# Two of four weight sums moved from VectorE to GpSimd, and two groups of loads moved along the sync queue, in an attention and MLP kernel

## Chip, cores and metric

The kernel runs on one core of one Trainium2 chip. The time is device microseconds of one execution. Executions are marked fast or slow: slow means over 1.5% above the fastest of the same kernel. A profiled execution also has a span, from its first to its last instruction, some 1.7 us below its time.

## The reference, cut to what matters

Eight batches ("groups") of 8 heads, 576 queries of 64, keys and values averaged over 8 rows; softmax; then an MLP with a tanh GELU over all 4608 tokens.

```python
k_p = k.reshape(B, H, Sp, 8, D).mean(axis=3)         # Sp = 72
v_p = v.reshape(B, H, Sp, 8, D).mean(axis=3)
attn = softmax(scale * q @ k_p.T)                    # 576 x 72 a head
x = (attn @ v_p) ... reshape(4608, 512)
h = x @ w_in                                         # 512 x 2048
g = 0.5 * h * (1 + tanh(c * (h + 0.044715 * h**3)))
out = g @ w_out                                      # 2048 x 512
```

## The kernel before

TensorE runs one MLP of 512 tokens after another: groups 0 to 6, then the "remainder" (64 tokens of each group), then group 7. I call these steps 0 to 8. While step n runs, ScalarE, VectorE and GpSimd prepare the attention of the group of step n+1, and the sync queue loads the group after that. Work is placed by hooks: `at(hooks, s, f)` calls f just before the s-th matmul of a step, and each engine runs its instructions in the order of these calls.

From step 1 on, the second half of the MLP is a fast 2x2 block product with 7 products in place of 8. It needs four sums of blocks of w_out, made once, the first at the end of step 0 and the others at the start of step 1, and sums of the activations in each step:

```python
def w_sums(which, m0, m1, eng):
    b11, b12, b21, b22 = [wq[:, m0:m1, i, HN * h:HN * h + HN] for i in range(2) for h in range(2)]
    t = [tw[:, i, m0:m1] for i in range(4)]
    in0, in1 = [(b12, b11), (b22, t[0]), (b22, b12), (b21, t[1])][which]
    eng.tensor_tensor(out=t[which], in0=in0, in1=in1, op=ALU.subtract)    # L405, 128x2048 bf16
```

What stands beside it on VectorE, and the loads:

```python
def pool(b, c0, c1):                        # averages K or V: three additions a call, L147 to L149
    ...
def finish(g, r, o, eng):                   # step 0's result out of PSUM, which frees a bank
    ...
    copy(eng, osb, o); store(g, r, osb)
# sync queue, within a step:
#   keys' transpose (L199), queries' transpose (L220), loads, four weight transposes eT (L294)
at(hooks, nj, norm, n, j, nc.gpsimd if j == 1 else nc.vector)
at(hooks, nj, e_transpose_dma, n, j)
...
at(hooks, 64 + 105, values, n, [nc.scalar, nc.vector])      # TensorE needs all four eT here, L326
```

PSUM holds TensorE's results, in banks that are copied out before TensorE uses them again. The sums of the activations are L411 to L414, the softmax is L252 (row sums), L261, L267. L360 and L472 are the two matrix products, L236 the scores, L421 the first matmuls of a step.

The softmax here doesn't subtract the row's maximum and nothing guards it: scores larger than these inputs give would overflow.

## Time and profile before

The median of the three runs was 286.09 us (285.46 to 286.67). The profile that came with them: 289.0 us, span 287.3. The table gives the length of the steps, as the distance between the first weight loads of L421 in TensorE's timeline, and TensorE's waits within them.

| profile of before (slow) | from start | step 1 | step 2 | step 3 | steps 4 and 5 |
|---|---|---|---|---|---|
| length, us | 52.06 | 30.32 | 30.66 | 29.53 | 28.43 each |
| TensorE's waits, us | | 0.82 scores, 1.02 values | 1.77 values | half clock | none |

A step without waits takes 28.43 us. The lines that carry this are in the prediction.

### The profile page before, as it was taken

Reading aid. Unit: us, or ns where it says so; the run is one execution under the profiler, and the core shown is the slowest. Engines: PE = TensorE matmul, PEld = TensorE weight load, DVE = VectorE, ACT = ScalarE, POOL = GpSimd, SP = SyncE. Lnnn points to the kernel's source line nnn. Section 1 sums busy time; section 2 is a strip of 40 time slices with the busy share of each in tenths; the row PEclk is TensorE's granted clock in tenths of the full one; section 3 lists DMA queues with packets and bytes.
Section 4 is the critical chain, followed back from the end, with each engine's and each line's share of the span. In section 5 each row is a group of like instructions: output and inputs, shape, how many; then the busy total and the mean of one; then the engine's idle time right before and its main releaser. Section 6 shows DMA issues by size and latency. Waiting matters only on the chain.

```text
span 287.3 us, 6029 instructions
## 1 busy us (share of the span) xinstructions
PE 276.0 (96%) x2430; PEld 176.4 (61%) x2430; DVE 200.2 (70%) x361; ACT 168.2 (59%) x264; POOL 58.1 (20%) x91
## 2 busy tenths in 40 slices
PE   8889999998989997999999999999999999999994
PEld 3678844446844683448745864586458845864583
DVE  4882868987867984499679966996699435844521
ACT  1586574787446852676467646763776377637620
POOL 4740272002400340031203120312031200100000
PEclk9999999999999998999999999999999999999999
DMA  7999999999989998696689868946813730253013
GB/s 227 303 186 281 373 385 179 325 328 258 197 236 255 308 175 192 216 347 73 157 221 349 131 158 222 283 55 154 235 48 43 168 104 0 48 119 75 1 40 111
DMA packets 71759, 54.34 MB, mean 189 GB/s; under 512 B 45618, under 2 KB 57906, under 8 KB 71730
## 3 DMA queue, kind: packets, MB, share of 16 engines
q1 hardware_dynamic: 69474, 51.72, 70.2%
q0 software_dynamic: 2112, 2.10, 4.6%
q8 instruction: 19, 0.31, 0.5%
q10 hardware_dynamic: 144, 0.13, 0.1%
q14 instruction: 10, 0.08, 0.1%
HBM read 36.70 MB, written 9.44 MB: 161 GB/s over the span
## 4 chain that ended last, share of the span: by engine, by line
PE 78%; DMA 4%; DVE 3%; issue 1%
PE mm L360 32%; PE mm L472 31%; PE mm L421 5%; PE xo L326 3%; PE x L472 2%; DMA eT<-eb 2%; PE sc L236 2%; DMA qT<-q_b 2%; DVE eb L267 1%; DVE den L252 1%; PE xo L335 1%; PE mm L376 0%; DVE r L261 0%; DVE kv L147 0%; DVE kv L148 0%
## 5 line engine op out<-in xcount | busy, mean ns | idle before, releaser
L360 PE MATMUL mm<-xT,w_in_b 128*128 128x512 bf16 x448 | 98.0, 379 | 0.0
L362 ACT ACTIVATE gT<-mm 128x512 bf16<-128x512 f32 x112 | 66.9, 598 | 27.8 <-PE mm L360 27.7
L360 PEld LDWEIGHTS <-w_in_b 128*128 128x128 bf16 x448 | 43.7, 98 | 52.9
L472 PEld LDWEIGHTS <-gT 128*128 128x128 bf16 x512 | 48.5, 98 | 10.4 <-issue 2.5
L169 POOL TENSOR_TENSOR vbd<-kvb,vmask 128x256 bf16<-128x256 bf16 (+2 forms) x40 | 23.0, 597 | 96.6 <-DVE kvb L149 55.7
L472 PEld LDWEIGHTS <-stage 128*128 128x128 bf16 x384 | 37.5, 98 | 4.4
L411 DVE TENSOR_TENSOR stage<-gT 128x512 bf16<-128x512 bf16 (+1 forms) x31 | 15.6, 503 | 21.4 <-ACT gT L362 21.2
L472 PE MATMUL mm<-tw,gT 128*128 128x256 bf16 x240 | 30.4, 276 | 0.0
L472 PE MATMUL mm<-w_out_b,gT 128*128 128x256 bf16 x240 | 29.9, 273 | 0.0
L88 ACT CAST xT<-xo 128x1024 bf16<-128x1024 f32 (+1 forms) x11 | 10.2, 935 | 32.7 <-PE xo L326 28.0
L252 DVE TENSOR_REDUCE den<-e 128x8 f32<-128x576 f32 x36 | 26.5, 736 | 3.2 <-ACT e L245 2.9
L88 ACT COPY osb<-mm 128x512 f32<-128x512 f32 x30 | 17.6, 588 | 17.3 <-PE mm L472 17.0
L472 PE MATMUL mm<-tw,stage 128*128 128x256 bf16 x224 | 26.7, 273 | 0.0
L147 DVE TENSOR_TENSOR kv<-kv 128x1024 f32<-128x1024 f32 (+3 forms) x19 | 21.3, 1119 | 7.6 <-DMA kv<-in_k_dram 5.1
L245 ACT ACTIVATE e<-sc 128x576 f32<-128x576 f32 x36 | 21.8, 649 | 6.0 <-PE sc L236 4.4
L267 DVE TENSOR_TENSOR eb<-e,r 128x576 bf16<-128x576 f32 x25 | 20.8, 831 | 0.9
L412 DVE TENSOR_TENSOR gT<-gT 128x512 bf16<-128x512 bf16 (+1 forms) x31 | 14.6, 470 | 8.9 <-ACT gT L362 7.6
L90 DVE CAST xT<-xo 128x1024 bf16<-128x1024 f32 (+1 forms) x9 | 10.0, 1106 | 15.0 <-PE xo L326 11.4
L267 POOL TENSOR_TENSOR eb<-e,r 128x576 bf16<-128x576 f32 x7 | 8.1, 1150 | 56.5 <-ACT e L245 56.5
L90 POOL CAST q_b<-q_sb 128x1024 bf16<-128x1024 f32 (+1 forms) x13 | 13.6, 1067 | 20.1 <-DMA q_sb<-in_q_dram 20.0
L421 PE MATMUL mm<-xT,w_in_b 128*128 128x512 bf16 x64 | 16.3, 400 | 0.1
L371 PE MATMUL mm<-xT,w_in_b 128*128 128x256 bf16 x128 | 15.6, 273 | 0.1
(84 smaller groups left out, 288.9 us busy)
## 6 DMA issues: line engine op xcount, KB each, us to landing
kv<-in_k_dram SPq DMA_DIRECT2D x7, 1024.0 KB, 6.7
q_sb<-in_q_dram SPq DMA_DIRECT2D x7, 1024.0 KB, 11.3
kv<-in_v_dram SPq DMA_DIRECT2D x6, 1024.0 KB, 9.4
out_dram<-osb SPq DMA_DIRECT2D x12, 512.0 KB, 3.0
kv<-in_v_dram SPq DMA_DIRECT2D x4, 512.0 KB, 10.8
w_in_b<-in_moe_w_in_dram POOLq DMA_DIRECT2D x4, 512.0 KB, 6.7
w_out_s<-in_moe_w_out_dram SPq DMA_DIRECT2D x2, 1024.0 KB, 13.7
stage<-in_moe_w_out_dram SPq DMA_DIRECT2D x2, 1024.0 KB, 14.9
```

The costliest lines, as they stand in the source:

```text
L88: eng.copy(out=out, in_=in_)
L90: eng.tensor_copy(out=out, in_=in_)
L147: add(out=t[:, :, 0:4, :], in0=t[:, :, 0:4, :], in1=t[:, :, 4:8, :], op=ALU.add)
L169: eng.tensor_tensor(out=vbd[p0:128, b, n0:n1, :].rearrange("p (c r) (hh d) -> p c (r hh) d", c=max(m, 1), d=D), in0=kvb[p0:128, 4 + c0:4 + ...
L245: nc.scalar.activation(out=e.rearrange("p (x h) s -> p x (h s)", x=2), in_=sc[:, :, 0:4 * Sp], func=ACT.Exp, scale=1.0 / 64.0)
L252: nc.vector.reduce_sum(out=den, in_=e, axis=AX.X)
L267: eng.tensor_tensor(out=o.rearrange("p (pr hh s) -> p hh pr s", hh=2, s=Sp), in0=e.rearrange("p (hh pr) s -> p hh pr s", hh=2), in1=r.rear ...
L360: nc.tensor.matmul(out=hp, lhsT=w_in_b[:, ko, fo * 128:(fo + 1) * 128], rhs=st[g]["xT"][:, ko, :], start=(i == 0), stop=(i == KO - 1))
L362: nc.scalar.activation(out=gT[:, fo, :], in_=hp, func=ACT.Gelu_apprx_tanh)
L371: nc.tensor.matmul(out=hp[:, f, :], lhsT=w_in_b[:, ko, (fo + f) * 128:(fo + f + 1) * 128], rhs=st[g]["xT"][:, ko, c0:c0 + 256], start=(ko ...
L421: nc.tensor.matmul(out=hp[f], lhsT=w_in_b[:, ko, f * 128:(f + 1) * 128], rhs=st[g]["xT"][:, ko, :], start=(ko == 0), stop=(ko == 3))
L472: nc.tensor.matmul(out=xs[p] if acc is xs else acc[:, p, :], lhsT=lt, rhs=rt, start=bool(fresh and m == 0 and (p == 0 or (last and acc is ...
```

## The change

Its intent: VectorE is busy without a break where the four sums stand, and its work leads to the scores and values of step 1; two sums go to GpSimd, which is idle there. The queries' transpose of group 3 stood behind a load of V in the sync queue; V goes behind it. Two of the remainder's small query loads leave step 2.

```diff
     at(hooks, 185, w_sums, 0, 0, NP, nc.vector)
+    at(hooks, 187, w_sums, 2, 0, NP, nc.gpsimd)
 ...
         if n_ == 1:
-            for i in range(1, 4):
-                at(hooks, i, w_sums, i, 0, NP, nc.vector)
+            at(hooks, 1, w_sums, 1, 0, NP, nc.vector)
+            at(hooks, 2, w_sums, 3, 0, NP, nc.gpsimd)
 ...
                 at(hooks, 45, load_kv, n2, (0,))
-                at(hooks, 64 + 52, load_kv, n2, (1,))
+                at(hooks, 64 + 100, load_kv, n2, (1,))
 ...
-        if 2 <= n_ <= 5:
-            at(hooks, 58, load_q, R, n_ - 2, n_ - 1, nc.sync)
+        for j in {3: (0,), 4: (1, 2), 5: (3,)}.get(n_, ()):
+            at(hooks, 58, load_q, R, j, j + 1, nc.sync)
```

## The prediction

> **What bounds the kernel now.** I read the page first: TensorE is busy 96% of the span, and no other engine is near it.
>
> ```profile
> PE 276.0 (96%) x2430; PEld 176.4 (61%) x2430; DVE 200.2 (70%) x361; ACT 168.2 (59%) x264; POOL 58.1 (20%) x91
> PEclk9999999999999998999999999999999999999999
> ```
>
> So a change off TensorE can win only TensorE's gaps. The kernel runs one MLP per group, and the next group's attention is prepared beside it; I call these steps. In the chain that ended last, in order of time, the quiet steps 4 and 5 (142.84 to 171.27, 171.27 to 199.70) take 28.43 us each. Steps 1 and 2 are longer (52.28 to 82.68 is 30.40, 82.68 to 113.25 is 30.57). The chain names the gaps in them (start, length, what):
>
> ```profile
> 62.66 4.80 DMA qT<-q_b
> 67.46 0.04 issue
> 67.51 0.46 PE sc L236 x32
> ...
> 71.29 8.29 PE mm L472 x75
> 79.58 1.02 issue
> 80.60 1.18 PE xo L326 x16
> ...
> 106.78 2.59 DMA eT<-eb
> 109.37 1.50 issue
> 110.87 1.18 PE xo L326 x16
> ```
>
> The reader is to see three waits: 0.82 us before the scores at 67.51 (for the transposed queries), 1.02 us before the values at 80.60, and 1.77 us before the values at 110.87 (TensorE's timeline gives 0.82, 1.02 and 1.77). Both values waits end just after the last transposed weights land: issued at 77.80 and 108.10, each 2.6 us to landing in the view of that line. The windows view shows a second price of the longest gap:
>
> ```profile
> 108.82:112.24 3.42, 1.65 (x22) 0.55 (x20) 0.16 (x2) 0.35 (x1) 0.00 (x0) 1.00 0.76 207
> 112.24:115.65 3.41, 3.41 (x13) 1.57 (x11) 3.34 (x4) 1.25 (x2) 0.00 (x0) 0.50 1.01 233
> ```
>
> After 3.42 us in which TensorE was busy only 1.65, the clock (third figure from the end) was 0.50 for 3.41 us. That costs half of 3.41, 1.7 us. All that this change can win is therefore 1.02 + 1.77 + 1.7 and perhaps 0.82, together 5.3 us of 286, below 2%.
>
> The weight sums stand on VectorE's timeline (start, length), and the evidence on what GpSimd does to VectorE is in the last two lines and GpSimd's before them:
>
> ```profile
> 49.06 0.97 POOL L169 TENSOR_TENSOR vbd<-kvb,vmask 128x256 bf16<-128x256 bf16 x2 [1.41 <-DVE kvb L149]
> ...
> 50.10 1.21 DVE L405 TENSOR_TENSOR tw<-w_out_b 128x2048 bf16<-128x2048 bf16 x1
> 51.61 0.69 DVE L90 COPY osb<-mm 128x512 f32<-128x512 f32 x1 [0.30 <-PE mm L376]
> 52.22 1.22 DVE L405 TENSOR_TENSOR tw<-w_out_b,tw 128x2048 bf16<-128x2048 bf16 x1
> ...
> 73.11 1.15 POOL L267 TENSOR_TENSOR eb<-e,r 128x576 bf16<-128x576 f32 x1 [6.24 <-ACT e L245]
> ...
> 73.87 1.01 DVE L267 TENSOR_TENSOR eb<-e,r 128x576 bf16<-128x576 f32 x1
> 75.88 0.76 DVE L267 TENSOR_TENSOR eb<-e,r 128x576 bf16<-128x576 f32 x1
> ```
>
> **What the Trainium skill says.** (1) "SBUF — State Buffer", Who interferes with whom: a VectorE instruction with two SBUF inputs contends with a GpSimd instruction that reads SBUF, and the one that issues first holds the shared ports for its whole length. The trace agrees: VectorE's product at 73.87 took 1.01 against 0.76, as if it began 0.25 later, at 74.11, about 0.15 before GpSimd's (73.11 + 1.15 = 74.26) ended. (2) "GPSIMD Engine Reference", 3.1 Elementwise: two-input work on GpSimd takes about twice VectorE's time (4497 against 2293 ns at 2048 fp32). This trace gives less: in the groups by form the 128x576 product takes 1150 ns and the undisturbed 128x256 spread 612, so 1.68 ns an element and 0.18 fixed. (3) "DMA: Bandwidth & Descriptors", Two DMAs through the same engine are not ordered: within a queue descriptors start in order. Here the landings follow the issues of the sync queue, so a small transpose waits for loads ahead of it. (4) "TensorE: Matmul & The Clock Gate", Part 1: the clock halves after an idle window of 3.4 us; the 0.50 for 3.41 us above agrees, though here 48% busy was already too little.
>
> **Part 1: two weight sums to GpSimd.** VectorE loses 2 x 1.22 = 2.44 us (the instructions at 53.35 and 54.49). GpSimd gains two of 0.18 + 2048 x 1.68 ns = 3.6 us each; it is idle from 50.03 to 58.65, so its own time is free. The question is the lock.
> - The third sum needs only the converted weights, done at 45.5, so it starts when GpSimd is free, at about 50.0, some 0.1 before VectorE's first sum at 50.10. It holds the ports to 50.0 + 3.6 - 0.15 = 53.45. VectorE's first sum then ends at 53.45 + 1.21 = 54.66 and not 51.31. Behind it stands the copy at 51.61, which frees the PSUM bank that TensorE wants at 54.00: it now ends near 55.3, and TensorE stalls 1.3 us.
> - The second sum follows, to 56.4. The fourth needs it and is ready at about 56.45, when VectorE's first pooling addition (1.49 us, at 55.62 before) has just begun, to 57.8. The fourth takes the ports at 57.67, to 61.13. The second addition ends at 61.96, the pooled keys are done at 62.8, against 58.86 before.
> - From there: four product sums to 65.4 (2.6 us), V's pooling to 67.8 (2.4), the spread keys to 68.7, eight product sums (3.4) to 72.1. The softmax begins at 72.1 against 70.31, since some 1.9 us of VectorE's idle time is used up. The last transpose lands 1.75 later, at 82.15. TensorE reaches the values at 79.58 + 1.3 + 0.3 and waits about 1.1 again. **Step 1 ends 1.75 later.**
> - If VectorE wins the first race instead, its first sum is undisturbed, the second is blocked to 54.63, and the rest goes alike with no bank stall: 1.2 later. I take **+1.4**.
>
> **Part 2: V of group 3 behind the query transpose.** Before, the sync queue went like this (start, length of issuing):
>
> ```profile
> 79.08 0.59 SPq L108 DMA_DIRECT2D kv<-in_v_dram  x1
> 79.77 0.45 SPq L392 DMA_DIRECT2D out_dram<-osb  x1
> 80.32 7.01 SPq L220 DMA_TRANSPOSE qT<-q_b  x1
> ...
> 92.04 0.51 SPq L120 DMA_DIRECT2D q_sb<-in_q_dram  x1
> 92.59 5.05 SPq L124 DMA_DIRECT2D q_r<-in_q_dram  x2
> 101.15 8.18 SPq L294 DMA_TRANSPOSE eT<-eb  x4
> ```
>
> The transpose blocked the queue 7.01 us behind V, against 2.93 to 3.40 in other steps, and the loads of group 4 went out from 89.57. Now the transpose takes some 3 us, V follows at once (7.1 us to landing before), and the loads of group 4 are issued about 1.9 earlier against TensorE's work. V lands near 92.3, and VectorE pools it at 91.68 + 1.4 = 93.1: narrow, no wait.
>
> **Part 3: the remainder's queries from step 3 on.** The two that leave step 2 stood just ahead of its transposes: issued at 92.6 and 96.5, landed 13.6 and 10.2 later, at 106.2 and 106.7, and the first transpose at 107.3 though issued at 101.15. The queue issued the last one at 108.10 although its data was there at 105.63 (74.80 to 75.88 is the same run of instructions in step 1). Without them (1.0 us of the queue) and with part 2 (0.9), the last transpose can be issued when its data is ready and lands before TensorE asks. **Step 2 loses its gap: -1.77.** The half clock after it goes too. The gate looks at fixed windows of 3.41 us, so a gap of 1.77 fills enough of one in perhaps half of the executions, an estimate: 0.5 x 1.7 = **-0.8** in the median. Step 4 gets four of these small loads where it had two. Its first transpose landed at 165.5, the last at 168.9, and TensorE came at 169.28: 0.4 of slack against 1 us more in the queue, partly hidden: **+0.3**. Steps 3 and 5 keep what they have.
>
> Sum: 286.09 + 1.4 - 1.77 - 0.8 + 0.3 = 285.2.
>
> **Rivals.** (a) The ports are not held against VectorE so long, or GpSimd starts late enough. Then VectorE gains up to 2.4 us in step 1, the 1.02 us wait shrinks to 0.3 (the transposes also stand behind K of group 3, landing at 77), and the total is 286.1 - 0.7 - 1.8 - 0.8 + 0.3 = 283.1. That the change was thought worth making speaks for it; the 1.01 against 0.76 above speaks against. (b) The blocked VectorE stalls TensorE long enough to halve its clock in step 1 as well, 1.7 us more, and V lands late for its pooling: about 287. A stall of 1.3 is below the 1.77 that did it. (c) The transfers are only rearranged and the step 2 gap stays in part: 286 to 287; against it, 1 us of loads really leaves the queue ahead of the transposes.
>
> **Range and chances.** The rivals span 283.1 to 287, the spread of the runs is 1.2 us: 282.7 to 287.0. Faster by 2% would need 5.7 us, more than all gaps that the parts touch; slower by 2% needs two clock losses on top of my worst sum. Hence 0.03, 0.95, 0.02.
>
> **What would show it.** GpSimd's two sums of about 3.6 us from 50.0; VectorE's first or second sum, and a pooling addition, stretched by 2 to 3.4 us; TensorE idle near 54; the values of step 1 later than 80.60. In step 2: a query transpose issued in about 3 us, the last transpose landing before TensorE's values, no gap there and no 0.50 after it. I am wrong if VectorE's sums and additions keep their 1.2 and 0.8 us, or if step 2 keeps a gap over 0.5 us.

## The result, and the profile after

The changed kernel takes 289.26 us (288.34 to 290.11, 4 runs); the kernel before, in the same rounds, 286.38. Ratios are the mean time of one kernel's fast runs over that of the other's of the same rounds, so not quite the ratio of the medians: 1.0104, with a 95% interval of 1.0061 to 1.0147. The change costs 3 us, and the time lies outside my range of 282.7 to 287.0. The profile is of a fast execution (288.34 us, span 286.6).

First TensorE's timeline (start, length, what, and in brackets the idle time before it and what ended it): steps 1 and 2.

```profile
55.47 12.25 PE L360 MATMUL mm<-xT,w_in_b 128*128 128x512 bf16 x55 [1.62 <-DVE osb L90]
69.82 0.45 PE L236 MATMUL sc<-kbd,qT 64*64 64x72 bf16 x32 [1.67 <-DMA qT<-q_b]
81.47 1.16 PE L472 MATMUL mm<-tw,gT 128*128 128x256 bf16 x9 [0.56 <-DVE osb L457]
83.28 1.18 PE L326 MATMUL xo<-eT,vbd 32*64 32x512 bf16 x16 [0.66 <-issue]
...
111.71 1.18 PE L326 MATMUL xo<-eT,vbd 32*64 32x512 bf16 x16
```

Step 1 has four waits, 4.51 us together, where in the slow profile of before it had two of 1.84. Step 2 has none. The steps are now 33.32, 28.42, 28.42 and 28.43 us. Next GpSimd's and VectorE's timelines of step 1's beginning:

```profile
49.67 4.07 POOL L405 TENSOR_TENSOR tw<-w_out_b 128x2048 bf16<-128x2048 bf16 x1
56.63 5.25 POOL L405 TENSOR_TENSOR tw<-w_out_b,tw 128x2048 bf16<-128x2048 bf16 x1 [2.89 <-DVE tw L405]
```

```profile
49.78 5.04 DVE L405 TENSOR_TENSOR tw<-w_out_b 128x2048 bf16<-128x2048 bf16 x1
54.74 0.68 DVE L90 COPY osb<-mm 128x512 f32<-128x512 f32 x1
...
57.99 4.57 DVE L148 TENSOR_TENSOR kv<-kv 128x640 f32<-128x640 f32 x1
...
73.88 0.75 DVE L252 TENSOR_REDUCE den<-e 128x8 f32<-128x576 f32 x1
```

The reader is to see the two long VectorE instructions, which took 1.21 and 0.82 before. The first began 0.11 after GpSimd's sum and ended 1.08 after it, so it began its own 1.2 us of work only when GpSimd was nearly done. The copy at 54.74, which frees the PSUM bank, came next, and TensorE waited for it from 53.85 to 55.47. The second is the addition that GpSimd's other sum overtook: that sum shows 5.25 us, of which about 1.2 was its own waiting for the addition before.

Last the sync queue of step 2, which did as the prediction said: the queries' transpose is issued in 3.29 us and not 7.01, V behind it.

```profile
82.52 3.29 SPq L220 DMA_TRANSPOSE qT<-q_b  x1
85.86 0.57 SPq L108 DMA_DIRECT2D kv<-in_v_dram  x1
...
90.21 0.57 SPq L108 DMA_DIRECT2D kv<-in_k_dram  x1
```

From one profile of each kernel the account would read: step 1 +3.00, steps 2 and 3 -3.35, and 0.3 less before step 1, so the changed kernel's span is 0.7 us shorter. Its time is 3 us longer. One of the two profiles cannot be typical, and the first question for the chip was which.

### The profile page after: what moved, and what is told of

Same layout as the page of the kernel before. It is cut to its first block, busy times and chain, and to the rows that moved or that the text cites. A ratio compares the mean times of both kernels' runs of the same rounds, so it can differ in the third digit from the quotient of the medians.

```text
span 286.6 us, 6011 instructions
## 1 busy us (share of the span) xinstructions
PE 273.7 (95%) x2412; PEld 176.0 (61%) x2430; DVE 206.8 (72%) x359; ACT 168.2 (59%) x264; POOL 67.5 (24%) x93
## 4 chain that ended last, share of the span: by engine, by line
PE 79%; DVE 17%; issue 2%; ACT 0%; DVEq 0%; POOL 0%; POOLq 0%
PE mm L360 29%; PE mm L472 29%; PE mm L371 5%; PE mm L421 4%; PE x L472 2%; DVE kv L148 2%; DVE den L252 2%; PE xo L326 2%; DVE tw L405 2%; DVE eb L267 2%; PE warm L571 2%; PE sc L236 2%; DVE kv L147 2%; DVE eb L279 1%; DVE stage L411 1%
## 5 line engine op out<-in xcount | busy, mean ns | idle before, releaser
L360 PE MATMUL mm<-xT,w_in_b 128*128 128x512 bf16 x440 | 97.6, 379 | 2.0 <-DVE osb L90 1.6
L169 POOL TENSOR_TENSOR vbd<-kvb,vmask 128x256 bf16<-128x256 bf16 (+2 forms) x40 | 23.6, 612 | 84.9 <-DVE kbd L90 44.4
L88 ACT COPY osb<-mm 128x512 f32<-128x512 f32 x30 | 17.6, 588 | 15.9 <-PE mm L472 15.5
L267 DVE TENSOR_TENSOR eb<-e,r 128x576 bf16<-128x576 f32 x25 | 21.7, 867 | 0.9
L148 DVE TENSOR_TENSOR kv<-kv 128x512 f32<-128x512 f32 (+3 forms) x19 | 16.1, 849 | 0.7
```

The lines of the kernel that those rows point to most:

```text
L88: eng.copy(out=out, in_=in_)
L148: add(out=t[:, :, 0:2, :], in0=t[:, :, 0:2, :], in1=t[:, :, 2:4, :], op=ALU.add)
L169: eng.tensor_tensor(out=vbd[p0:128, b, n0:n1, :].rearrange("p (c r) (hh d) -> p c (r hh) d", c=max(m, 1), d=D), in0=kvb[p0:128, 4 + c0:4 + ...
L267: eng.tensor_tensor(out=o.rearrange("p (pr hh s) -> p hh pr s", hh=2, s=Sp), in0=e.rearrange("p (hh pr) s -> p hh pr s", hh=2), in1=r.rear ...
L360: nc.tensor.matmul(out=hp, lhsT=w_in_b[:, ko, fo * 128:(fo + 1) * 128], rhs=st[g]["xT"][:, ko, :], start=(i == 0), stop=(i == KO - 1))
```

## The experiments

**The theory.** GpSimd's sums hold VectorE off (a VectorE instruction that starts beside one does its own work only when that one ends) for their whole length; step 1 lengthens by 3 us; the gain of the moved loads in step 2 is not in ordinary executions. **The rival.** The moved loads do the harm: V of group 3 comes late, or four small loads in step 4 delay its transposes.

**1. The kernel before, once more.** No edit.

> The kernel before, once more, for a second profile of it. Ratio 1.000 within 0.004. What is asked is step 2 (from the start of one MLP to the start of the next): if the 1.77 us wait before the values of step 2 is in ordinary executions too, this profile shows step 2 at about 30.2 us (28.43 + 1.77) and step 3 at 28.4 when the clock is not halved. If that wait belonged to the one slow profile, step 2 is 28.4 to 29.4, and the gain that I promised to parts 2 and 3 was never there.

Measured: ratio 0.9987 (0.9965 to 1.0009), the profile fast, 284.35 us. Step 1 is 29.67 us, step 2 is 28.43. TensorE's timeline:

```profile
66.93 0.46 PE L236 MATMUL sc<-kbd,qT 64*64 64x72 bf16 x32 [0.90 <-DMA qT<-q_b]
...
79.30 1.18 PE L326 MATMUL xo<-eT,vbd 32*64 32x512 bf16 x16 [0.29 <-issue]
...
107.72 1.18 PE L326 MATMUL xo<-eT,vbd 32*64 32x512 bf16 x16
```

The wait of 1.77 us in step 2 is not there, nor the half clock after it. They belonged to the one slow profile. The queries' transpose stood behind V here too and was issued in 6.49 us (7.01 in the slow profile), so this long issue does not by itself make TensorE wait. What I meant to win in step 2 was, in this execution, nothing.

**2. Part 1 alone, and 3. parts 2 and 3 alone.** The edits are the first two and the last two places of the diff above.

> Only the two weight sums go to GpSimd; the loads stay as in the kernel before. Theory (GpSimd's long two-input instructions hold VectorE off): step 1 takes 33.0 to 33.6 us against 30.3, VectorE's first sum about 5.0 us and its second pooling addition about 4.6 us, ratio 1.009 to 1.018. Rival (the moved loads did the harm): ratio below 1.004 and step 1 under 31.5.

> Only the loads are moved; all four weight sums stay on VectorE. Theory: step 1 stays at 30.3 us and step 2 is 28.4 without a gap; ratio 0.994 if step 2's 1.77 us wait is there in ordinary executions of the kernel before, 1.000 if it is not. Rival (the moved loads did the harm): ratio above 1.004.

Measured: part 1 alone 1.0121 (1.0097 to 1.0145), step 1 33.31 us. Parts 2 and 3 alone 0.9982 (0.9963 to 1.0001), step 1 29.81. The product of the two, 1.0103, is the whole change's 1.0104. The rival falls: the harm is part 1. Parts 2 and 3 are within noise of nothing; by the interval they win 1.1 us at most. They did not even keep step 2 free of waits, though no remainder's query was in its way:

```profile
108.71 1.18 PE L326 MATMUL xo<-eT,vbd 32*64 32x512 bf16 x16 [0.69 <-DMA eT<-eb]
```

This wait scatters with either order of loads. With the old one it was 1.77, 0, 0.47 (part 1 alone), 0.75 (experiment 8) and 0 (experiment 11); with the new one 0, 0.69, 0.90, 0, 0.29, 0.65 and 0 (the changed kernel and experiments 3 to 7 and 10). The means are 0.60 and 0.36, from single profiles, the slow one among them; without it the old order has 0.31.

**4. The copy that frees the bank, on ScalarE.**

```diff
-            finish(g, r, o[r], nc.scalar if r == 3 else nc.vector)
+            finish(g, r, o[r], nc.scalar if r >= 2 else nc.vector)
```

> The changed kernel, with the third copy of step 0's result (the one that stood behind VectorE's held first sum and freed TensorE's PSUM bank) on ScalarE. If the lateness of step 1 is VectorE's chain, the 1.6 us stall at the start of step 1 goes but the waits for queries, sums and values grow by nearly as much: step 1 at 32.3 to 33.0 us, 0.3 to 1.0 less than the changed kernel's 33.3. If the stall itself is what costs, the whole 1.6 is won: step 1 at 31.7 us.

Measured: ratio 1.011 (1.0088 to 1.0133), step 1 32.83 us. The stall of 1.62 is gone, and the wait before the scores grew from 1.67 to 2.69:

```profile
68.89 0.63 PE L236 MATMUL sc<-kbd,qT 64*64 64x72 bf16 x32 [2.69 <-DMA qT<-q_b]
```

By these two profiles 0.5 us of step 1 hung on the stall itself; the times do not show it (1.011 against 1.0104). The rest is VectorE's lateness, which TensorE meets at the next place that needs it. The wait is put down to a DMA, but VectorE stands behind it: its copy L162 ended at 62.81, the keys' transpose was issued at 62.84, and the queries' transpose only behind that in the queue, at 64.50, though ScalarE's last conversion of the queries had ended at 62.16.

**5. GpSimd writes only.** Each of its sums is replaced by two fills with zeros of the same tile. The result is wrong.

```diff
-    at(hooks, 187, w_sums, 2, 0, NP, nc.gpsimd)
+    for _ in range(2):
+        at(hooks, 187, nc.gpsimd.memset, tw[:, 2], 0.0)
```

(The fourth sum likewise, with `tw[:, 3]`.)

> The changed kernel, but GpSimd, in place of each of the two sums, writes zeros twice into the same tile: it writes and reads nothing of SBUF. The result is wrong on purpose. If VectorE is held because both instructions READ through the shared interface, VectorE's first sum is back at 1.2 us and its second pooling addition at 0.8, step 1 takes 29.2 to 29.8 us and the ratio is 0.994 to 1.000. If any long GpSimd instruction beside VectorE does it (or the mere order of the instructions), step 1 stays above 31 us.

Measured: ratio 0.9992 (0.9965 to 1.0019), step 1 30.19 us. GpSimd's four fills ran from 49.54 to 56.82 without a break. GpSimd's line, VectorE's and then TensorE's timelines:

```profile
49.54 7.28 POOL L658 MEMSET tw<- 128x2048 bf16 x4
```

```profile
49.67 1.21 DVE L405 TENSOR_TENSOR tw<-w_out_b 128x2048 bf16<-128x2048 bf16 x1
...
54.87 1.49 DVE L147 TENSOR_TENSOR kv<-kv 128x1280 f32<-128x1280 f32 x1 [1.83 <-DMA kv<-in_v_dram]
56.39 0.82 DVE L148 TENSOR_TENSOR kv<-kv 128x640 f32<-128x640 f32 x1
```

```profile
67.12 0.45 PE L236 MATMUL sc<-kbd,qT 64*64 64x72 bf16 x32 [0.83 <-DMA qT<-q_b]
...
80.07 1.18 PE L326 MATMUL xo<-eT,vbd 32*64 32x512 bf16 x16 [0.87 <-DMA eT<-eb]
```

Two things follow. VectorE is not held by 7.3 us of GpSimd instructions that only write, so the hold comes with GpSimd's reading. And this kernel is part 1 at its best: VectorE is rid of two sums and of every hold in this stretch, and nothing is won that can be told from noise (by the interval 1.0 us at most). It stands 1.83 us before its first pooling addition, which waits for a load, and 1.04 before it copies the transposed keys; TensorE's two waits (0.83 and 0.87) are no shorter than in experiment 1 (0.90 and 0.29). Both name a transfer. Step 1 missed my 29.2 to 29.8, I take it for that reason.

**6. The same two sums in eight pieces each.**

```diff
-    at(hooks, 187, w_sums, 2, 0, NP, nc.gpsimd)
+    for m in range(NP):
+        at(hooks, 187, w_sums, 2, m, m + 1, nc.gpsimd)
```

(The fourth sum likewise.)

> The changed kernel, but each of GpSimd's two sums cut into eight of 128x256 (about 0.65 us each, so more GpSimd time in all). If the ports are held for one whole instruction at a time and then go to the other engine that waits, no VectorE instruction is held longer than about 0.6 us: no stall at the start of step 1, step 1 at 30.6 to 31.8 us, ratio 1.002 to 1.006. If it is GpSimd's total time that VectorE loses, step 1 stays at 33.

Measured: ratio 1.0063 (1.0042 to 1.0084), step 1 31.84 us, at the upper edge of the expectation. VectorE's timeline:

```profile
49.99 1.64 DVE L405 TENSOR_TENSOR tw<-w_out_b 128x2048 bf16<-128x2048 bf16 x1
...
56.40 1.17 DVE L148 TENSOR_TENSOR kv<-kv 128x640 f32<-128x640 f32 x1
...
58.48 0.61 DVE L162 COPY kvb<-kvb 128x320 bf16<-128x320 bf16 x1
```

Each VectorE instruction is held by part of a piece (0.43 and 0.35 us in the first two lines in place of 3.83 and 3.75), the stall at the bank is gone. The two engines take turns, instruction by instruction: the ports are held for one instruction and then go to the one that waits. But the pieces took GpSimd 17.6 us in all, with its waiting, and VectorE's two-input instructions pay again and again; the last line shows that a copy with one input pays too (0.61 us in place of 0.26). So it is still slower than doing the sums on VectorE.

**7. Only the third sum on GpSimd, and 10. only the fourth.** In the first, `nc.gpsimd` of `w_sums, 3` becomes `nc.vector`; in the second, the third sum goes back to VectorE ahead of the fourth.

> The changed kernel with the fourth sum back on VectorE; only the third is on GpSimd. It sizes the two holds apart. Held-ports theory: VectorE's first sum about 5.0 us and the stall of 1.6 us at the start of step 1 stay, the second pooling addition is back at 0.8 us; VectorE is 2.5 us earlier than in the changed kernel and meets its waits: step 1 at 30.7 to 31.5 us, ratio 1.002 to 1.007.

> The changed kernel with the third sum back on VectorE; only the fourth is on GpSimd. The other half of the sizing. Held-ports theory: no stall at the start of step 1, all VectorE sums 1.2 us, but the fourth is ready while VectorE's third runs, takes the ports next and holds the first pooling addition for about 3.8 us (1.5 becomes about 5.2). VectorE ends 2.5 us later than in the kernel before, less what its idle time absorbs: step 1 at 30.5 to 31.5 us, ratio 1.002 to 1.006.

Measured: third only 1.0042 (1.0018 to 1.0066), step 1 31.85, a little over the expectation; VectorE's first sum 5.03 us, the stall of 1.62 is there, its additions take 1.48 and 0.83. Fourth only 1.0041 (1.002 to 1.0061), step 1 31.14. There GpSimd waited for VectorE's third sum and then held the first addition; its line, then VectorE's:

```profile
53.05 4.91 POOL L405 TENSOR_TENSOR tw<-w_out_b,tw 128x2048 bf16<-128x2048 bf16 x1 [3.55 <-DVE tw L405]
```

```profile
54.45 4.86 DVE L147 TENSOR_TENSOR kv<-kv 128x1280 f32<-128x1280 f32 x1 [0.41 <-DMA kv<-in_v_dram]
```

That addition takes 1.49 us alone. Each hold by itself costs 0.4%, both together 1.0% (the changed kernel; all three have parts 2 and 3 as well). Against parts 2 and 3 alone (0.9982), each costs 0.6% and both 1.2%. So the two holds add up within the noise; that VectorE's slack swallows a share of the first is not shown.

**8, 9 and 11. What does set step 1?** If VectorE's sums are not on the path in the kernel before, the waits before scores and values should yield to moved transfers. All three start from the kernel before.

Experiment 8, earlier conversion of the queries that are transposed for step 1's scores:

```diff
-                    at(hooks, 28 + 4 * j, cast_q, n, j, j + 1, nc.scalar)
-                at(hooks, 41, q_transpose_dma, n)
+                    at(hooks, [28, 32, 32, 32][j], cast_q, n, j, j + 1, nc.scalar)
+                at(hooks, 33, q_transpose_dma, n)
```

> A version meant to beat both: the kernel before, with three of the four conversions of the queries for step 1's scores one to two units earlier on ScalarE. The wait for the transposed queries (0.8 to 0.9 us in both profiles of the kernel before) should go, for they are issued about 1 us earlier: step 1 at 28.5 to 29.5 us against 29.7 to 30.3, ratio 0.995 to 0.999. If VectorE's chain or the loads set the values' time anyway, the wait before the values grows by as much and the ratio is 1.000.

Missed: ratio 0.999 (0.9965 to 1.0015). The transpose was issued at 61.66, about 1 us earlier, and took 5.9 us to land against 4.8; the wait before the scores is 0.95.

Experiment 9, the queries' loads behind the weight transposes:

```diff
-                s2 = 44 if n_ == 1 else 57
+                s2 = 64 + 52
```

> The kernel before, with each load of a later group's queries (1 MB) issued behind the four weight transposes of a step and not ahead of them. Asks what the waits before the values hang on. If it is transfers ahead of the transposes in the sync queue, the waits before the values go in step 1 (0.3 to 1.0 us before) and in step 2 (0 to 1.8 us before): step 1 at 29.0 to 29.5 us, step 2 at 28.4, ratio 0.994 to 0.998, unless the later queries hold GpSimd's conversion and with it the queue. If VectorE sets the values' time, step 1 stays at 29.7 to 30.3.

Half right: step 1 falls to 28.92 us and its wait before the values is gone, so, as far as one profile shows it, that wait hangs on transfers ahead of it (in the other profiles of the old order it was 0.29 us or more). But the ratio is 1.0042 (1.0025 to 1.006): steps 2 to 5 grow to 29.67, 28.86, 29.13 and 29.35. The queries come later (those loaded in step 1 landed at 83.44, in the slow profile of before at 71.97), GpSimd converts them later (to 86.00), and the sync queue, which issues in order, holds all that follows; the transpose of the queries goes out at 86.03, where the store ahead of it was issued at 78.99. Sync queue and TensorE of step 2:

```profile
78.99 0.41 SPq L392 DMA_DIRECT2D out_dram<-osb  x1
86.03 2.79 SPq L220 DMA_TRANSPOSE qT<-q_b  x1
```

```profile
108.82 1.18 PE L326 MATMUL xo<-eT,vbd 32*64 32x512 bf16 x16 [1.18 <-DMA eT<-eb]
```

Experiment 11, experiment 8 with two of step 0's four stores behind the queries' transpose:

```diff
-        store(g, r, osb)
+        late.append((g, r, osb)) if r >= 2 else store(g, r, osb)
 ...
+                for one in late:
+                    at(hooks, 34, store, *one)
```

> The version with earlier conversions, and two of step 0's four stores (0.5 MB) issued behind the query transpose and not ahead of it. In the run with earlier conversions the transpose was issued 1 us earlier and landed no earlier (5.9 us after its issue against 4.8). If transfers ahead of it in the queue are the reason, it now lands at least 0.9 us earlier against the start of step 1 and the wait before the scores (0.95 us) shrinks below 0.3; the wait before the values may grow, as 0.5 MB moves ahead of the weights' transposes: step 1 at 29.0 to 29.9 us. If the transpose waits for the keys' transpose or for something else, the 0.95 stays.

Missed: ratio 1.0022 (1.0002 to 1.0043). The transpose took 5.8 us and the wait stayed at 0.86, so taking the stores out from ahead of it did not bring it sooner. They were issued at 63.07 and 64.12, while it was still on its way, so they may have slowed it from behind. The wait before the values rose to 1.73, step 1 to 31.08. What delays the queries' transpose stays open. None of the kernels tried beats the kernel before by more than noise.

## Why the prediction was wrong, point by point

The median came out 4.06 us over the point. **The mechanism of part 1 was right; its size was not (step 1 longer by 3.65 us and not 1.4), and of the 2.6 us of gain set against it ordinary executions have about 0.5.** Two steps failed: the sizing of step 1, and the reading of one slow profile as the ordinary case.

1. *"The third sum ... starts when GpSimd is free, at about 50.0, some 0.1 before VectorE's first sum"*: right (49.67 and 49.78). Experiments 5 and 6 show the hold for what it is.
2. *"0.18 + 2048 x 1.68 ns = 3.6 us each"*: wrong by 0.47 us each, 4.07 measured. I took the rate from products with f32 inputs and from masked spreads. The hold lasted 3.83 us and not 3.35, TensorE's stall 1.62 and not 1.3.
3. *"From there: ... eight product sums (3.4)"*: they took 4.26 (69.70 to 73.96), for GpSimd's spreads of V fell beside them and held three of them (0.73, 0.65 and 0.50 in place of 0.42). Such holds stand in the trace of before, at 94.96 to 96.98, and I left them out. The four product sums ahead took 3.1 and not 2.6. From VectorE's first sum to the softmax I had 72.1 - 50.1 = 22.0 us; measured 73.88 - 49.78 = 24.1. The two longer sums are 0.94 of this, the product sums 1.4.
4. *"Step 1 ends 1.75 later ... I take +1.4"*: measured 3.00 against the slow profile (33.32 and 30.32), 3.65 against the fast one (29.67). The waits were 1.62, 1.67, 0.56 and 0.66; I had 1.3, 1.1, none and 1.1. The third is a new one: VectorE's late addition reads a PSUM bank that TensorE wants to accumulate in.
5. *"Step 2 loses its gap: -1.77"* and *"0.5 x 1.7 = -0.8"*: this is the step that turned the sign. The trace that I read was of an execution of 289.0 us, 1% above the median. The second profile of the same kernel has no wait in step 2 and no half clock, and parts 2 and 3 alone bring 0.18%, half a microsecond, with an interval from 1.1 us to nothing. I spread 2.6 us of gain over a median that had little of it to lose. The wait scatters from 0 to 1.77 us with the old order and from 0 to 0.90 with the new; its cause in one execution I cannot name.
6. *"Step 4 ... +0.3"*: 28.43 us in the changed kernel, no wait. In one of the experiments (5) step 4 had 0.48.

In sum: +2.25 for step 1 (3.65, fast profile against fast, where I had 1.4), +2.1 for the gain (half a microsecond in experiment 3 where I had 2.6), -0.3 for step 4, some 4.05. Measured are 4.06, of which 0.29 is the kernel before, which took 286.38 and not 286.09 in these rounds. That it fits so well is partly luck, as the step lengths are from single profiles.

The rivals fare no better. Rival (a) supposed that a VectorE that is not held would win 0.7 us in step 1; experiment 5 is that case, and it wins nothing. The trace of before shows VectorE waiting 1.02 us for the keys' transpose, and I had named the transposes that stand behind K of group 3, and still reckoned with a VectorE-bound step. Rival (b)'s second half clock did not come in the profile, but it was near: the least busy stretch of 3.42 us in the changed kernel (67.73 to 71.15) had TensorE busy for 1.75 us, and 1.65 was followed by half clock in the slow profile. Other executions probably had it, an inference: the mean granted clock was 0.991 to 0.994 in 8 of the 20 executions of the four kernels with both sums on GpSimd (the changed one, there the run of 290.11 us, and experiments 2, 4 and 6), and 0.996 or more in all other fast executions; one stretch of 3.41 us at half clock takes 0.006 off. Their times are not consistently longer (287.94, the fastest of experiment 4, is one of them), and no trace of them was kept. Rival (c), a step 2 gap that stays in part, is nearest to what parts 2 and 3 did, but it had step 1 at 1.4 too.

What the prediction asked to be shown in step 1 came: sums of about 4 us from 49.7, two stretched VectorE instructions (by 3.83 and 3.75 us, more than the 2 to 3.4 foretold), TensorE idle near 54 and a later end of the step. In step 2 the queries' transpose was issued in 3.29 us; that no gap stood there was luck, as experiment 3 has one of 0.69 with the same loads.

## What to carry to other kernels

Before work is moved off an engine, show that its end is what the next engine waits for: here VectorE was busy without a break, and freeing it of 2.4 us won nothing beyond noise, for it then waited for a load and a transpose. GpSimd is no free help for VectorE's two-input work: where VectorE had such work at the same time, a sum that takes VectorE 1.21 us cost it up to 3.83 us when GpSimd did it. And a wait seen in one profile is a sample: a profile 1% over the median calls for a second one before its gaps are counted as gains.

## What the Trainium skill lacked or had wrong

- "GPSIMD Engine Reference", 3.1 Elementwise, gives fp32 alone (4497 against 2293 ns at 2048, 1.96 times). For bf16 with two inputs of 128x2048 the runs show 4.07 us on GpSimd against 1.21 on VectorE, 3.4 times; the "roughly 2×" at the head of the page would mislead here.
- "SBUF — State Buffer", Who interferes with whom, holds in the runs here: 7.3 us of GpSimd instructions that only write held nothing, sums that read held VectorE 3.83 and 3.75 us. It does not say who comes next when both engines queue instructions: with pieces of 0.67 us (by themselves) they took turns one by one, and VectorE's 1.2 us sum became 1.64.
- "TensorE: Matmul & The Clock Gate", Part 1, speaks of an idle window of 3.4 us and does not say how idle. In the slow profile 1.65 us busy in 3.42 was followed by a clock of 0.50; in experiment 4 a stretch of 3.50 us with 0.81 busy (65.40 to 68.90) was followed by 1.00. That fits windows at fixed places, which the page states: laid out in steps of 3.41 us from where the clock records of each trace begin, experiment 4's gap is split between two windows with 1.99 and 2.15 us busy. On this grid no window with 1.75 us or more (the changed kernel's least) was followed by half clock before the end of the program.
- No page says how far DMA waits scatter from one execution to the next in one kernel: 0 to 1.77 us at the same place in two profiles of the kernel before.
